# Early up-projections: the high part behind a group's first exponentials, the low part at the start of its second call

## The chip, the cores and the metric

One core of one Trainium2 chip runs the whole program. The metric is device time in microseconds (us) of one execution; the median of the runs counts. TensorE is called PE, its weight loads PEld, VectorE DVE, ScalarE ACT, GpSimd POOL, SyncE SP.

## What is computed

Attention with a band of 32 and 32 global rows over 4 batches of 8 heads, then two MLPs of 2304 tokens, width 512 and hidden width 2048:

```python
s_ll = np.where(np.abs(pos[:, None] - pos[None, :]) <= 32, scale * q_l @ k_l.T, -1e9)
a_l = sm(concat([scale * q_l @ k_g.T, s_ll]))       # local rows: global keys and a band
out_l = a_l @ concat([v_g, v_l])
out_g = sm(scale * q_g @ k_all.T) @ v_all            # global rows: all keys
x = concat([out_g, out_l]).reshape(2304, 512)        # heads side by side
h = x @ w_in;  x = where(h > 0, h, exp(min(h, 0)) - 1) @ w_out          # first MLP
h = x @ w_in2; x = where(h >= 1, h, where(h <= -1, 0, (h + 1)**2 / 4)) @ w_out2
```

## The kernel before

The MLP products are made with operands split into a high and a low part (xh and xl for activations, wh and wl for weights, gh and gl for the hidden layer), three products in place of one. The high part is a copy by ScalarE, the low part the difference to it by VectorE, so a low part always follows its high part.

The first stage, attention, is a loop of calls n = 0 to 25 over 24 units in groups of three: a local unit (one pair of heads of a batch), a global unit (the global rows of four heads), a local unit. Counted from 0, n divisible by 3 is a group's first call. A call issues the steps of three units at once: scores, maxima (top) and exponentials (expo) of unit n; transposes (turn: tiles pt or tg), their copies by ScalarE (copy: pT or pgT) and the products with the values (values: po or pog) of unit n - 1; division (norm on VectorE: den, then o_sb or og), transposes back on PE (back: ot or tg3) and the split into xh and xl (high on ScalarE, low on VectorE) of unit n - 2. Maxima read the scores in PSUM and write sn (with nml) for a local unit, m and nm for a global one; exponentials of a global unit read the scores (sg) in PSUM straight and write pg. Two PSUM banks hold scores, three the transposes, one the values.

All instructions of this stage are pinned: each engine runs its own in the order of the text. The order within a call is that of lines 733 to 750: scores(n), norm(n-2), turn(n-1), copy(n-1), back(n-2), high(n-2), top(n), low(n-2), expo(n), a step of weight preparation (wraw to top, rest, power, wh, wl) from n = 4 on, values(n-1), then loads (arrive).

Five up-projections of the first MLP run within this stage from n = UP_AT = 8 on, by a generator that is stepped twice a call: at its start (line 734) and ahead of the values (line 747). One up-projection takes 12 matmuls (six at n = 8, six at n = 9), the curve on ScalarE (exponential, then the Relu) at the start of n = 10, the join on VectorE late in n = 10, the high part gh on ScalarE at the start of n = 11 and the low part gl on VectorE late in n = 11. The next one begins in that same step, so the pattern repeats every three calls, n = 11 being a group's third call. The five share one PSUM bank, which the join frees. gh and gl come from pools of five buffers, g from one of two.

After the loop the engines are no longer pinned; the rest of the first MLP and the second MLP follow, planned by due times (later, catch_up), nearly all matmuls of lines 247 and 320. Down-projections of batch 0 are issued within n = 24 already, on the first three early results. In the profile, L113 is the helper that pins an instruction, so instructions of the first stage are told apart by their tiles.

Of the kernel before, what the change touches and what calls it, by code (L numbers as in the profile page):

```python
# [20 lines left out]
B, H, SL, SG, D = 4, 8, 512, 32, 64  # L21
# [9 lines left out]
KT = DM // P  # L31
# [14 lines left out]
UP_EARLY = 5  # L46
# [4 lines left out]
UP_AT = 8  # L51

UP_STEP = 6
# [13 lines left out]
def band_attention_then_two_mlps(  # L67
# [77 lines left out]
    chunks = []  # L145
    for layer in range(2):
        f = 0
# [164 lines left out]
    def down(layer, fs, j, f, gs, banks, ds):  # L312

        gh, gl = gs
        wh, wl = (w[:, KT * P:] for w in wtiles[layer, f])
        for d in ds:
            if f == fs[0]:
                banks[d] = ps_dn[d // 2].tile([P, SL], F32, tag=f"dn{d}", name="dn")
            for k, (w, g) in enumerate(((wl, gh), (wh, gh), (wh, gl))):
                eng.tensor.matmul(  # L320
                    banks[d],
                    w[:, d * P:(d + 1) * P],
                    g,
                    start=f == fs[0] and k == 0,
                    stop=f == fs[-1] and k == 2,
                )
            if f == fs[-1]:
                collect(layer, fs, j, d, banks[d])
# [40 lines left out]
    def mpool(name, bufs, **kw):  # L369
        return ctx.enter_context(tc.tile_pool(name=name, bufs=bufs, reuse_waits="tile", **kw))  # L370
# [6 lines left out]
    with ExitStack() as actx:  # L377
# [298 lines left out]
        def early_weights():  # L676

            for part in parts:
                for _ in range(3):
                    next(part, None)  # L680
                    yield

        def early_ups():

            for f, j in [(f, j) for j in range(B) for f in chunks[0][1]][:UP_EARLY]:
                u = Up(0, f, j)
                u.products(UP_STEP)
                yield
                yield
                u.products(3 * KT - UP_STEP)  # L690
                yield
                u.curve()
                yield
                u.join()
                yield
                u.high()
                yield
                u.low()

        parts = [prep(g_p, wtmp_p, 0, *part, raw_tag="wraw") for part in halves]  # L700
        sent = iter(parts)
        weights, ups = early_weights(), early_ups()

        def part(n, name):

            if 0 <= n < len(units):
                if n not in live:
                    live[n] = units[n][0](*units[n][1:])
                live[n][name]()

        def arrive(n):

            g, r = divmod(n, 3)
            p = 2 * g + 1
            if r == 1 and p + 1 < len(pairs):
                load_qk(*pairs[p + 1])
            elif r == 2 and p + 2 < len(pairs):
                load_qk(*pairs[p + 2])
            elif r == 0 and g:
                next(next(sent, iter([0])))  # L720
            while ahead and len(ahead) > 2 * len(pairs) - V_UNTIL.get(n, 4 * g + (4, 6, 7)[r]):
                load_v(*ahead.pop(0))
            if r == 0 and g and p < len(pairs):
                spread_queries(*pairs[p])
            elif r == 1 and p < len(pairs):
                spread_keys(*pairs[p])
            elif r == 2 and p + 1 < len(pairs):
                spread_keys(*pairs[p + 1])
# [1 line left out]
        ahead = [(*pair, (e,)) for pair in pairs[1:] for e in range(2)]  # L730
        live, first = {}, {}
        for n in range(len(units) + 2):
            if n > UP_AT:
                next(ups, None)
            part(n, "scores")
            part(n - 2, "norm")
            part(n - 1, "turn")
            part(n - 1, "copy")
            part(n - 2, "back")
            part(n - 2, "high")  # L740
            part(n, "top")
            part(n - 2, "low")
            part(n, "expo")
            if n >= PREP_AT:
                next(weights, None)
            if n >= UP_AT:
                next(ups, None)
            part(n - 1, "values")

            arrive(n)  # L750
            if n == len(units):

                s_ctx.close()
                ps_dn.append(mpool("ps_dn0", 1, space=PSUM))
                for f in chunks[0][1]:
                    down(0, chunks[0][1], 0, f, made[0, f, 0], first, range(KT // 2))
        for _ in weights:
            pass
        for _ in ups:
            pass  # L760
        prep_ctx.close()
        eng = free
# [13 lines left out]
    step = 0  # L776
# [24 lines left out]
    for ci, (layer, fs) in enumerate(chunks):  # L801
# [3 lines left out]
        for i, (j, f) in enumerate(order):  # L805
            if j == GR:
                u = Up(layer, f, j)
# [88 lines left out]
```

## Time and profile before

| | us |
|---|---|
| median of 3 runs (lowest to highest) | 861.51 (860.61 to 861.84) |
| the profiled execution, own time | 859.64 |
| its span, first to last instruction | 857.8 |
| PE busy in the span | 842.2 |
| VectorE busy | 580.6 |
| ScalarE busy | 431.7 |
| GpSimd busy | 27.0 |

Times in the rows count from the span's start. In a timeline a row is a run of like instructions on one engine; a bracket at its end is the engine's idle time just before it and the instruction that ended it. Matmul ends are modelled. The granted TensorE clock is full (1.00) in all stretches.

### The profile page before, as it was taken

What the parts mean: (1) busy time and instruction counts of PE and PEld (TensorE: products, weight loads), DVE (VectorE), ACT (ScalarE), POOL (GpSimd) and SP (SyncE); (2) the same over time, 40 slices, a digit from 0 to 9 for tenths busy, and PEclk for the clock granted to TensorE, in tenths of its full rate; (3) what the DMA queues carried; (4) which work ended last, traced back from release to release, by engine and by line L of the source; (5) the groups of instructions that cost most, each with busy time, mean ns of one, the idle gap of its engine ahead of it and who ended that gap; (6) DMA issues with size and microseconds to landing.
All of it is one profiled execution on the core that took longest, in us unless ns stands there. A gap on an engine that the chain in (4) does not pass through costs nothing.

```text
span 857.8 us, 14902 instructions
## 1 busy us (share of the span) xinstructions
PE 842.2 (98%) x6138; PEld 691.9 (81%) x6138; DVE 580.6 (68%) x1130; ACT 431.7 (50%) x755; POOL 27.0 (3%) x66
## 2 busy tenths in 40 slices
PE   8899999999999999999999999999999999999998
PEld 5677778888888888888888888888888888888886
DVE  5888857879437954734499896369759754845455
ACT  5778766765335534433456664355435333433332
POOL 2231200000000000000000000000000000000000
PEclk9999999999999999999999999999999999999999
DMA  8988712322101210200021112012102100000014
GB/s 278 305 267 266 239 47 99 105 92 99 50 1 49 99 50 1 98 1 1 1 98 50 50 64 84 1 50 99 49 1 80 69 0 1 1 1 0 2 62 147
DMA packets 23124, 65.45 MB, mean 76 GB/s; under 512 B 3984, under 2 KB 4240, under 8 KB 19344
## 3 DMA queue, kind: packets, MB, share of 16 engines
q1 hardware_dynamic: 22768, 64.23, 22.0%
q8 instruction: 48, 0.79, 0.4%
q10 hardware_dynamic: 288, 0.26, 0.1%
q14 instruction: 20, 0.16, 0.1%
HBM read 60.03 MB, written 4.46 MB: 75 GB/s over the span
## 4 chain that ended last, share of the span: by engine, by line
PE 96%; DMA 2%; issue 1%; ACT 1%; DVE 0%; SPq 0%
PE dn L320 40%; PE up L247 39%; PE up L244 3%; PE dn L337 3%; PE s L113 2%; PE po L113 2%; PE up L113 2%; PE pt L113 2%; PE sg L113 1%; PE pog L113 1%; PE tg L113 1%; DMA wraw<-in_w 1%; DMA v_sb<-in_vwin 1%; PE ot L113 1%; PE dn L113 1%
## 5 line engine op out<-in xcount | busy, mean ns | idle before, releaser
L320 PE MATMUL dn<-gh,wh 128*128 128x512 f32 x506 | 196.9, 389 | 0.0
L320 PE MATMUL dn<-gl,wh 128*128 128x512 f32 x506 | 196.8, 389 | 0.0
L320 PE MATMUL dn<-gh,wl 128*128 128x512 f32 x506 | 196.3, 390 | 0.0
L247 PE MATMUL up<-xh,wl 128*128 128x512 f32 x492 | 192.5, 391 | 0.0
L247 PE MATMUL up<-xl,wh 128*128 128x512 f32 x492 | 191.6, 389 | 0.0
L247 PE MATMUL up<-xh,wh 128*128 128x512 f32 x492 | 191.6, 389 | 0.0
L278 ACT ACTIVATE gh<-g 128x512 fp32r<-128x512 f32 x123 | 77.7, 632 | 118.8 <-DVE g L267 71.8
L297 DVE TENSOR_TENSOR acc<-dn,acc 128x512 f32<-128x512 f32 x128 | 84.7, 684 | 48.6 <-PE dn L320 48.4
L320 PEld LDWEIGHTS dn<-gl,wh 128*128 128x128 f32 x506 | 95.0, 188 | 19.8
L320 PEld LDWEIGHTS dn<-gh,wh 128*128 128x128 f32 x506 | 95.0, 188 | 19.5
L320 PEld LDWEIGHTS dn<-gh,wl 128*128 128x128 f32 x506 | 95.0, 188 | 19.4
L282 DVE TENSOR_TENSOR gl<-g,gh 128x512 fp32r<-128x512 f32 x123 | 84.5, 688 | 38.6 <-ACT gh L278 37.6
L247 PEld LDWEIGHTS up<-xh,wh 128*128 128x128 f32 x492 | 92.3, 188 | 19.2
L247 PEld LDWEIGHTS up<-xh,wl 128*128 128x128 f32 x492 | 92.4, 188 | 18.8
L247 PEld LDWEIGHTS up<-xl,wh 128*128 128x128 f32 x492 | 92.4, 188 | 18.7
L258 ACT ACTIVATE g<-up,half_sb 128x512 f32<-128x512 f32 (+1 forms) x69 | 47.0, 681 | 113.4 <-PE up L247 104.5
L266 DVE SCALAR_TENSOR_TENSOR g<-g 128x512 f32<-128x512 f32 (+1 forms) x69 | 46.9, 679 | 59.3 <-ACT g L258 59.2
L264 DVE SCALAR_TENSOR_TENSOR g<-up,g 128x512 f32<-128x512 f32 x64 | 43.3, 677 | 61.8 <-ACT g L255 61.8
L253 ACT ACTIVATE g<-up 128x512 f32<-128x512 f32 x64 | 37.8, 591 | 85.9 <-PE up L247 80.5
L267 DVE TENSOR_TENSOR g<-g,e 128x512 f32<-128x512 f32 (+1 forms) x69 | 46.9, 679 | 3.6
L180 ACT ACTIVATE top<-wraw 128x1024 f32<-128x1024 f32 x29 | 33.6, 1159 | 29.9 <-DMA wraw<-in_w 19.8
L255 ACT ACTIVATE g<-g,one_sb 128x512 f32<-128x512 f32 x64 | 45.9, 717 | 1.8
(112 smaller groups left out, 916.8 us busy)
## 6 DMA issues: line engine op xcount, KB each, us to landing
wraw<-in_w SPq DMA_DIRECT2D x29, 1024.0 KB, 4.8
v_sb<-in_vwin SPq DMA_DIRECT2D x32, 520.0 KB, 5.1
k_sb<-in_kT SPq DMA_DIRECT2D x16, 288.0 KB, 4.4
q_sb<-in_qT SPq DMA_DIRECT2D x16, 272.0 KB, 5.0
outT<-acc SPq DMA_DIRECT2D x16, 256.0 KB, 2.1
wraw<-in_w SPq DMA_DIRECT2D x6, 512.0 KB, 5.9
outT<-acc_rows SPq DMA_DIRECT2D x4, 64.0 KB, 2.2
mask_sb<-in_mask ACTq DMA_DIRECT2D x1, 192.0 KB, 4.1
```

Of the source, the lines that this page charges most:

```text
L113: return lambda *args, **kw: tc.keep_in_program_order(fn(*args, **kw))
L247: eng.tensor.matmul(self.ps, w, x, start=k == 0, stop=k == 3 * KT - 1)
L253: eng.scalar.activation(self.g, self.ps, AF.Exp)
L255: eng.scalar.activation(self.g, self.g, AF.Relu, bias=one_sb, scale=-1.0)
L258: eng.scalar.activation(self.g, self.ps, AF.Relu, bias=half_sb, scale=0.5)
L264: eng.vector.scalar_tensor_tensor(g, self.ps, 0.0, g, ALU.max, ALU.subtract)
L266: eng.vector.scalar_tensor_tensor(g, g, 1.0, g, ALU.min, ALU.mult)
L267: eng.vector.tensor_tensor(g, g, self.e, ALU.add)
L278: eng.scalar.activation(self.gh, self.g, AF.Copy)
L282: eng.vector.tensor_tensor(self.gl, self.g, self.gh.bitcast(F32), ALU.subtract)
L297: eng.vector.tensor_tensor(a, ps, a, ALU.add)
L320: eng.tensor.matmul(banks[d], w[:, d * P:(d + 1) * P], g, start=f == fs[0] and k == 0, stop=f == fs[-1] and k == 2,)
```

## The change

The generator early_ups is replaced by a function up_work, which the loop calls at the same two places of each call with n and a flag (begin). It derives from n and each running up-projection's number k what is due. Products, curve and join stay in their calls. The high part moves from the start of call 11 + 3k to the later place in call 12 + 3k, behind the exponentials and the weight step of a group's first call. The low part moves from the later place in call 11 + 3k to the start of call 13 + 3k, a group's second call, ahead of the division of unit n - 2; there it also stands ahead of the curve of the next up-projection in the text. The next up-projection's products used to follow the low part; they now follow nothing of this kind.

```diff
-        def early_ups():
-
-            for f, j in [(f, j) for j in range(B) for f in chunks[0][1]][:UP_EARLY]:
-                u = Up(0, f, j)
-                u.products(UP_STEP)
-                yield
-                yield
-                u.products(3 * KT - UP_STEP)
-                yield
-                u.curve()
-                yield
-                u.join()
-                yield
-                u.high()
-                yield
-                u.low()
+        early = [(f, j) for j in range(B) for f in chunks[0][1]][:UP_EARLY]
+
+        def up_work(n, begin):
+
+            for k, u in running.items():
+                step = n - UP_AT - 3 * k, begin
+                if step == (2, True):
+                    u.curve()
+                elif step == (2, False):
+                    u.join()
+                elif step == (4, False):
+                    u.high()
+                elif step == (5, True):
+                    u.low()
+            k, r = divmod(n - UP_AT, 3)
+            if not begin and 0 <= k < len(early) and r < 2:
+                if r == 0:
+                    running[k] = Up(0, *early[k])
+                running[k].products(UP_STEP)
...
-        weights, ups = early_weights(), early_ups()
+        weights, running = early_weights(), {}
...
-            if n > UP_AT:
-                next(ups, None)
+            up_work(n, True)
             part(n, "scores")
...
-            if n >= UP_AT:
-                next(ups, None)
+            up_work(n, False)
             part(n - 1, "values")
...
-        for _ in ups:
-            pass
```

## Rows read from the trace of the kernel before

**Rows 1.** The page, parts 1 and 4: busy us by engine; the chain's shares.
```profile
PE 842.2 (98%) x6138; PEld 691.9 (81%) x6138; DVE 580.6 (68%) x1130; ACT 431.7 (50%) x755; POOL 27.0 (3%) x66
...
PE 96%; DMA 2%; issue 1%; ACT 1%; DVE 0%; SPq 0%
```

**Rows 2.** Busy time by stretch: stretch, length, busy us of each engine, clock, DMA.
```profile
200.00:250.00 50.00, 50.00 (x224) 41.41 (x223) 27.43 (x39) 20.14 (x31) 0.00 (x0) 1.00 0.12 42
```

**Rows 3.** Waits of PE, 55 to 116 us: us in total, times, longest.
```profile
PE s L113 <- issue: 3.3, 7, 1.1
PE s L113 <- ACT top L113: 1.6, 1, 1.6
```

**Rows 4.** The chain in order of time, third and second calls: start, us, what.
```profile
69.75 0.44 issue
...
72.07 0.63 PE ot L113 x4
...
82.46 0.44 PE ot L113 x4
82.89 1.05 PE po L113 x64
83.94 0.18 issue
84.12 0.97 PE s L113 x26
85.09 0.90 issue
...
100.67 1.06 issue
```

**Rows 5.** Timeline of ScalarE, end of n = 15 to n = 17: start, us, instruction.
```profile
80.33 0.62 ACT L113 ACTIVATE wh<-top 128x512 fp32r<-128x512 f32 x1
80.85 0.58 ACT L113 ACTIVATE g<-up 128x512 f32<-128x512 f32 x1
...
82.09 1.07 ACT L113 ACTIVATE pT<-pt 128x512 f32<-128x512 f32 x2
83.04 0.60 ACT L113 ACTIVATE xh<-ot 128x512 fp32r<-128x512 f32 x1
83.52 0.88 ACT L113 ACTIVATE pg<-sg,nm 128x272 f32<-128x272 f32 x2
...
86.06 0.63 ACT L113 ACTIVATE gh<-g 128x512 fp32r<-128x512 f32 x1 [1.09 <-DVE g L113]
87.47 0.87 ACT L113 ACTIVATE pgT<-tg 128x512 f32<-128x512 f32 x2 [0.78 <-PE tg L113]
```

**Rows 6.** Timeline of VectorE, end of n = 15 to the start of n = 18.
```profile
79.05 0.69 DVE L113 SCALAR_TENSOR_TENSOR wl<-rest,power 128x512 fp32r<-128x512 uint32 x1
80.34 0.17 DVE L113 TENSOR_SCALAR den<-po 128x8 f32<-128x8 f32 x1 [0.60 <-PE po L113]
...
80.78 0.69 DVE L113 TENSOR_TENSOR o_sb<-po,den 128x512 f32<-128x512 f32 x1
...
82.20 0.21 DVE L113 TENSOR_SCALAR nm<-m 128x1 f32<-128x1 f32 x1
...
91.00 0.69 DVE L113 TENSOR_TENSOR gl<-g,gh 128x512 fp32r<-128x512 f32 x1
91.61 0.14 DVE L113 TENSOR_SCALAR den<-pog 128x1 f32<-128x1 f32 x1
```

**Rows 7.** Timeline of VectorE: den in the second calls n = 13 and 22.
```profile
65.13 0.17 DVE L113 TENSOR_SCALAR den<-po 128x8 f32<-128x8 f32 x1 [0.54 <-PE po L113]
...
111.28 0.17 DVE L113 TENSOR_SCALAR den<-po 128x8 f32<-128x8 f32 x1 [0.68 <-PE po L113]
```

**Rows 8.** Timeline of PE's weight loads in n = 16.
```profile
82.82 0.95 PEld L113 LDWEIGHTS po<-v_sb,pT 128*32 128x32 f32 x64 [0.17 <-ACT pT L113]
```

**Rows 9.** The page, part 3: DMA queue and kind, packets, MB, share of 16 engines.
```profile
q8 instruction: 48, 0.79, 0.4%
```

## The prediction

> **What bounds the kernel now.** I read the page first, part 1 and the chain of part 4: TensorE (PE) is busy for 98% of the span, and the chain that ended last is 96% PE [rows 1]. Such an average hides stages, so next came the table by stretch. From 120 us on PE is full (200 to 250 us: 50.00 of 50.00) [rows 2]; the change touches nothing there, and what the attention stage before it loses or gains reaches the end whole. So only the stage with the unit loop matters, and in it the calls n = 11 to 25, where the five early up-projections run. There I read what PE waits for: from 55 to 116 us the view has just two rows, both in front of scores matmuls [rows 3]. PE waits for no high part, no low part and no pgT. Then I took one group, calls n = 15 (first, local unit), 16 (second, global unit) and 17 (third, local unit), and laid the chain [rows 4], ScalarE [rows 5] and VectorE [rows 6] beside each other. The reader is to see three things. In the third call ScalarE stands 1.09 us in front of gh, waiting for the join, and after gh it idles another 0.78 us until PE has made tg [rows 5]: gh has slack there. From the end of the first call through the second, ScalarE has none: wh, g, pT, xh and pg follow each other without an idle mark [rows 5]. And PE's scores of the third call wait for pg, which needs xh before it on its queue, which needs ot, which needs o_sb from VectorE's norm [rows 4 to 6].
>
> **What the change takes away.** Five times gh (0.63 us) leaves the third call's start on ScalarE, and with it the 1.09 us wait [rows 5]; five times gl (0.68 us, 0.61 us until the next starts) leaves the third call's end on VectorE [rows 6]. Gain on the path: 0. On ScalarE the next instruction, pgT, waits for PE's tg in any case; on VectorE the next is the norm of pog, and no PE wait for it is among [rows 3]. The cover is PE's own solid queue. Were it gone, the gain would be at most 0.63 us a group.
>
> **What it adds.** I follow k = 1; its gh now stands at the end of n = 15 behind the eight exponentials and wh, and its gl is the first VectorE work of n = 16, ahead of norm(14), where the curve of k = 2 follows on ScalarE. Nothing is issued on SyncE or GpSimd and no DMA is moved; PE's order is unchanged. gh and gl have five buffers for five units, g has two, so no new buffer wait.
> (1) wh starts at 80.33 and the next at 80.85 [rows 5]. So gh would run from 80.85 to 80.85 + 0.63 = 81.48, and g, pT come 0.52 later: pT at 82.61.
> (2) VectorE ends wl at 79.05 + 0.69 = 79.74 and now idles 0.60 us until den at 80.34 [rows 6]. gl doesn't fit into that idle time, since its gh ends only at 81.48. In order, it waits until then, and den follows 0.61 us behind: some 82.12, that is 82.12 - 80.34 = 1.78 us later. This is the added wait; queued behind it are norm(14) and top(16).
> (3) Everything of the norm shifts by 1.78: o_sb ends at 80.78 + 0.69 + 1.78 = 83.25, nm at 82.20 + 0.21 + 1.78 = 84.19 [rows 6].
> (4) PE runs ot(14) at 82.46 now, 0.99 us after o_sb was there (81.47) [rows 4, 6]; that slack pays for part of the 1.78. After the change ot can't begin before 83.25. How long it then takes no row shows at this place; the bounds are 0.44 us, as in the solid stream, and 0.63 us, as where it opened after tg at 72.07 [rows 4]. I take 0.63, since that one too begins after a break, plus an estimated 0.05 us for the signal: end at 83.93. po(15) follows it instead of 82.89: 1.04 later.
> (5) xh(14) was at 83.04, held by pT ahead of it. pT's shift would allow 83.56; ot allows 83.93. So +0.89, and pg 84.41 for 83.52, with nm (84.19) there in time [rows 5].
> (6) The scores of n = 17 start now at 84.12, 0.18 us after po, as pg frees their banks [rows 4]. They would start near 85.01 by pg, po being 1.04 later: the shift is 0.89 to 1.04, and I take **0.95 us** for one group. From 0.44 and no signal time at (4) comes xh at 83.69, a shift of 0.65, the lower end.
>
> If the VectorE part of this were hidden, ScalarE's would remain: po's weight load already waits 0.17 us for pT [rows 8], and pT comes 0.52 later. That is the lower price of the same mechanism, about 0.5 us a group.
>
> **The sum.** The pattern stands four times, den at 65.13, 80.34, 95.66 and 111.28, the first and the last in [rows 7]: n = 13, 16, 19, 22. After each, all that follows moves as one, since the third and first calls are led by PE, so it adds up: 4 x 0.95 = 3.8 us. The fifth pair (k = 4) lies at the end of n = 24 and the start of n = 25; no scores are left there, and on PE down-projection products stand between the last values and the last ot. I price it at 0, with 0.7 us (gl and its gap) as its upper end. The profiled execution's own time is 859.64 us, 857.8 of it span; it would become 863.4. It lies 1.87 below the median of the runs, 861.51, so I add the sum to the median: 861.51 + 3.8 = **865.3 us**.
>
> **Where a page speaks to it.** In three of the third calls the scores stop a second time, in mid-stream, for 0.44, 0.90 and 1.06 us, put down to "issue" and not to any engine [rows 4], while a queue of kind "instruction" brought 48 packets, 0.79 MB, over the run [rows 9]. The Trainium skill, Runtime: NRT & Kernel Launch, section Instruction fetch mechanics, says that instructions are refilled in blocks of 16 KiB while the block before runs, and that crossing a block is mostly hidden. The size agrees with this trace (0.79 MB / 48 is about 16 KB); hidden it doesn't look here, and by the page's rule the gaps would be something else, nothing could be made up in them, and the sum would stay 865.3.
>
> **The rivals.**
> *Caught up in the issue gaps.* If those gaps are late instructions whose delivery is already under way when PE stands before ot, the delivery goes on during the new stand and the gaps shrink. For it: they come in mid-stream, some 2 to 3 us behind ot, with no releaser. Against: PE has come through slow transposes before ot, so its queue is as full before the new stand as after it, and delivery is asked for at a place in the program that moves along. At most 0.44 + 0.90 + 1.06 = 2.4 us come back: 3.8 - 2.4 = +1.4, **862.9 us**. Chance 0.15.
> *Faster: the third call was ScalarE's.* If it is gh, not PE, that holds the third call (pgT behind gh, pog behind pgT), taking it out gives back up to 0.63 us in each of five groups, 3.2 us: **858.3 us**, provided that gl costs nothing. That turns on one point: gh must end by 79.74, so that gl falls into the 0.60 us in which VectorE idles. Against it: ScalarE's 0.78 us idle behind gh ends on PE's tg, and wh starts at 80.33 [rows 5]. Chance 0.07.
> *It doesn't do what it says.* The engines' order could differ from the text's, with gl behind the norm: then only the 0.5 us of ScalarE can be lost, and part of that in front of ot; near **861.5 us**, with up to 2 us more. Against: the order of the rows before is the text's, instruction for instruction. Chance 0.08.
>
> **How the numbers follow.** Forecast 0.70, the others 0.15, 0.07, 0.08. About 0.2% (1.7 us, here 859.8 to 863.2) is what a measurement of this kernel can tell from no change. Slower by more than that: the forecast, and a third of the case of the issue gaps (if they give back only part): 0.70 + 0.05 = 0.75. Same: 0.10 + 0.07 = 0.17. Faster: 0.08, the rival's 0.07 and one for the rest. The forecast's own bounds are 4 x 0.65 = 2.6 and 4 x 1.04 + 0.7 = 4.9 us, and the order of the free instructions behind the stage may shift the end by an estimated 1 us. The range leaves out the two cases at 861.5 and below, takes in that of the gaps: 862.2 to 867.4.
>
> **What would show it.** In the trace after: gl directly in front of den in the second call, with an idle mark "ACT gh" of about 1.7 us; den 1.8 us behind the end of po; a PE idle mark in front of ot in n = 13, 16, 19 and 22 released by VectorE; the third call's scores about 1 us later in each group, and the stage's end some 3.8 us later, with PE full behind it. ScalarE in the third call would idle in front of pgT for longer than the 0.78. I am wrong if ot has no wait, if den stands no further from the next group's than before, or if the issue gaps vanish.

## The result, and the profile after

The changed kernel takes 868.1 us (median of 6 runs, 866.99 to 870.27) beside 861.21 for the kernel before: ratio 1.0076, 95% interval 1.0062 to 1.0089. It is slower, as forecast, but by 6.6 us (by the ratio; 6.9 between the medians) and not by 3.8. Its profiled execution took 867.85 us, 866.0 of it span. Single executions that took 1054 to 1698 us are left out of all ratios below, and no median moves by more than 0.2 us for them.

I count the loss in one stretch, from the first scores of n = 12 to the first down-projection product; ahead of it lies of the change only that gh and gl of k = 0 are gone from n = 11. In the chain before they start at 60.06 and 124.32, after at 61.85 and 132.48: 64.26 and 70.63 us, so 6.37 more. Behind it both kernels run alike (TensorE full). The 1.79 us by which n = 12 itself comes later I don't put down to the change: these scores started at 61.94 us in a second profile of the kernel before, at 60.35 and 62.18 with one part moved, and at 63.46 in the changed kernel again. In this execution PE stood for 2.30 us ("issue") ahead of the scores of n = 11, where the kernel before had stood for 1.57, and then made them at half the granted clock (0.50 from 56 to 58 us) in 2.08 us for 1.26; the new work had not begun by then.

The chain that ended last, changed kernel, in order of time (start, us, what). It answers to [rows 4 to 6], with k = 1 from 84.00 on:

```profile
83.48 0.52 ACT wh L113
84.00 0.53 ACT gh L113
...
84.56 0.69 DVE gl L113
85.25 0.09 DVE den L113
...
85.60 0.70 DVE o_sb L113
...
86.43 0.64 PE ot L113 x4
...
87.10 0.61 ACT xh L113
...
87.73 0.69 DVE xl L113
88.42 0.78 DVE rest L113
...
89.22 0.69 DVE rest L113
89.92 0.60 DVE g L113
...
90.86 0.70 DVE o_sb L113
...
91.70 0.63 PE ot L113 x4
92.32 1.39 PE up L113 x6
...
94.80 1.09 PE s L113 x64
95.89 0.60 PE pt L113 x4
...
96.51 1.09 ACT pT L113 x2
...
97.71 2.32 ACT sn L113 x8
...
104.72 1.18 PE s L113 x40
105.90 2.20 issue
108.10 0.64 PE s L113 x24
...
122.40 1.40 PE s L113 x54
123.80 0.73 issue
```

Before, this chain was almost all PE. Now the first two groups close in themselves over three engines: exponentials, wh, gh, gl, norm, ot, xh, xl, rest, join, norm, ot, then PE's up, pog, scores and pt, then pT and the next exponentials. The new work is read in it directly: gh and gl (84.00 to 85.25). And late in it stand two stops in the scores, 2.20 us in n = 20 ([rows 4] had 1.06 there) and 0.73 in n = 23.

VectorE's timeline, changed kernel, start of the second call n = 16, and its waits from 55 to 124 us (engine, line, releaser: us in total, times, longest), then PE's:

```profile
84.56 0.69 DVE L113 TENSOR_TENSOR gl<-g,gh 128x512 fp32r<-128x512 f32 x1 [2.07 <-ACT gh L113]
85.17 0.16 DVE L113 TENSOR_SCALAR den<-po 128x8 f32<-128x8 f32 x1
```

```profile
DVE gl L113 <- ACT gh L113: 7.8, 4, 2.1
...
PE ot L113 <- DVE o_sb L113: 6.3, 6, 1.2
PE s L113 <- issue: 4.5, 2, 2.3
```

Four waits for gh, 7.8 us together; six waits of ot where [rows 3] had none: four in the second calls, and two in the third calls of n = 14 and 17. Of the two waits put down to issue one is the stop in n = 20, the other the 2.30 us ahead of n = 11, before the stretch; the stop in n = 23 ends behind this window.

### The profile page after: what moved, and what is told of

Read it like the earlier page. It is cut to its first block, busy times and chain, and to the rows that moved or that the text cites. A ratio compares the mean times of both kernels' runs of the same rounds, so it can differ in the third digit from the quotient of the medians.

```text
span 866.0 us, 14902 instructions
## 1 busy us (share of the span) xinstructions
PE 843.0 (97%) x6138; PEld 692.5 (80%) x6138; DVE 583.1 (67%) x1130; ACT 431.5 (50%) x755; POOL 29.2 (3%) x66
## 4 chain that ended last, share of the span: by engine, by line
PE 90%; ACT 3%; DMA 3%; DVE 2%; issue 1%; SPq 0%
PE dn L320 40%; PE up L247 39%; PE up L244 3%; PE dn L337 3%; PE s L113 2%; ACT sn L113 1%; DMA wraw<-in_w 1%; ACT pT L113 1%; PE pog L113 1%; PE up L113 1%; PE ot L113 1%; PE pt L113 1%; DMA v_sb<-in_vwin 1%; DVE o_sb L113 1%; PE po L113 1%
```

## The experiments

"Stretch" is the one defined above; "groups" are its four parts, each from the first scores of one group's first call to the next (the last to the first down-projection).

| kernel | us | ratio to before (interval) | stretch | groups |
|---|---|---|---|---|
| before | 861.2 | | 64.26 | 15.14, 15.37, 15.55, 18.21 |
| before again | 861.58, one run | | 64.31 | 15.12, 15.16, 15.55, 18.48 |
| changed | 868.1 | 1.0076 (1.0062 to 1.0089) | 70.63 | 16.40, 16.55, 17.68, 19.99 |
| changed again | 870.1 | 1.0093 (1.0073 to 1.0113) | 72.06 | 16.13, 16.81, 19.20, 19.92 |
| low part alone moved | 862.6 | 1.0004 (0.9989 to 1.0018) | 65.00 | 15.84, 15.12, 15.12, 18.92 |
| high part alone moved | 863.9 | 1.0022 (1.0010 to 1.0033) | 66.38 | 15.85, 15.63, 15.65, 19.25 |
| low part ahead of the join | 866.3 | 1.0051 (1.0034 to 1.0068) | 68.45 | 16.38, 15.74, 15.74, 20.59 |
| high moved, low ahead of the join | 866.7 | 1.0053 (1.0036 to 1.0070) | 69.77 | 16.94, 16.25, 16.94, 19.64 |
| VectorE stalled | 869.5 | 1.0085 (1.0066 to 1.0103) | 71.56 | 16.95, 16.88, 17.27, 20.47 |
| before, shifted by 40 | 864.9 | 1.0038 (1.0023 to 1.0053) | 64.59 | 15.88, 15.53, 15.23, 17.95 |
| changed, shifted by 40 | 868.1 | 1.0075 (1.0057 to 1.0092) | 68.73 | 16.41, 16.55, 16.87, 18.91 |
| changed, shifted by 14 | 867.9 | 1.0068 (1.0044 to 1.0093) | 72.52 | 16.85, 16.12, 19.40, 20.14 |
| short loop | 861.3 | 0.9984 (0.9966 to 1.0002) | 65.21 | 15.20, 16.00, 15.32, 18.69 |
| short loop, shifted by 52 | 867.0 | 1.0049 (1.0030 to 1.0068) | 66.70 | 16.14, 16.84, 15.68, 18.04 |

The stretch comes from one execution each, the time from several (but for "before again"). For the kernel shifted by 14 the stretch is from a further execution of 870.17 us.

**Which of the two moves costs?** Both parts in other places, against the changed kernel:

```diff
-                elif step == (5, True):
+                elif step == (5, False):
                     u.low()
```

> The changed kernel, but the low part is issued in the second call's later place, so behind the norm, the maxima and the exponentials, not ahead of them; the high part stays behind the first call's exponentials. Before: 861.2 us, changed: 868.1. Theory V (the loss is made by VectorE waiting for gh ahead of the norm): the mark 'gl <- ACT gh' is gone, den stands right behind po again, ot in the second call has no wait or one of at most 0.3 us, and the time is 861 to 863.5 us; what is left is ScalarE's 0.52 us a group. Rival S (the loss is gh's place on ScalarE, between the exponentials and the copies, where ScalarE has no idle time): 867 to 869 us, as in the changed kernel.

Measured: 866.7 us. gl waits for nothing and den follows po again, yet only a third of the loss is gone by the ratios, and 0.86 of 6.37 us of the stretch; I had expected 861 to 863.5. The time lies 0.3 us under the range of rival S (867 to 869), too little to decide on it; the high part alone does that below. The later place in the second call puts gl ahead of the join (at 89.55 in its chain, the join behind it at 90.15), so this kernel lengthened VectorE's way from xl to the third call's norm. That this way had no slack was the first sign that the picture of the third call was wrong. The parts had to be taken singly.

The low part alone at the start of the second call, the high part where it was before the change:

```diff
-                elif step == (4, False):
+                elif step == (3, True):
                     u.high()
```

> Only the low part is moved: it is the first VectorE work of the second call, as in the changed kernel, while the high part stays at the start of the third call, two calls earlier. Theory V: gh is long made, so gl falls into the 0.60 us in which VectorE idled for po; den moves by under 0.1 us; 860 to 862 us. Rival S expects the same. Rival P (gl's place ahead of the norm costs by itself, waiting or not): four times 0.6 us, 863.5 us or more.

862.6 us, 0.6 above the range, but with a ratio of 1.0004: no loss that can be measured. Rival P falls. gl's place ahead of the norm is free if gh is long made; it lies in VectorE's idle 0.60 us [rows 6]; behind gl at 82.17 VectorE still idles 0.26 us until den.

VectorE held up without touching ScalarE (against the changed kernel; the tile gl is allotted once):

```diff
-                elif step == (4, False):
+                elif step == (3, True):
                     u.high()
+                elif step == (3, False):
+                    u.low()
                 elif step == (5, True):
-                    u.low()
+                    for _ in range(4):
+                        u.low()
```

> High and low part where they were before the change; at the start of the second call VectorE makes the low part four times over (the same numbers into the same tile), waiting for nothing: 4 x 0.61 = 2.44 us from 79.74 on, so that den comes at 82.18, 1.84 us later than before, as in the changed kernel (1.78 by my working). ScalarE is left alone. Theory V: the same loss as the change, 866 to 869 us, with ot's wait for o_sb near 1 us in each group. Rival S: 861 to 863 us.

869.5 us, 0.5 above the range of theory V and far from that of rival S, which is no proof of V: four low parts are 9.8 us of VectorE work more over the stretch, the chain runs through VectorE nearly without a break, and the loss (7.3 us of stretch) is that of a full engine. It shows how little room VectorE has there.

**The loop.** After these I formed theory L: a loop through ScalarE and VectorE as long as PE's own group. Two kernels put one piece each into it. The high part alone (against the changed kernel; the fifth low part stays in n = 25):

```diff
-                elif step == (5, True):
+                elif step == (6, False) or (k, n) == (4, 25) and not begin:
                     u.low()
```

> The high part where the change puts it; the low part where it stood before within a call, the end of a third call, but one group later (the fifth in the second call n = 25), so VectorE's order in the second call and up to the third call's norm is as before the change. Theory L: only gh's 0.52 us lies in the loop, 4 x 0.52 = 2.1 us: 863.5 to 865 us. Theory of the prediction (PE leads the third call, slack pays for ScalarE's part): at most 0.5 us a group as well, but VectorE's share absent: 861.5 to 863.5.

863.9 us, as theory L has it, but only 0.4 above the other range, so the time doesn't decide. The groups say more: beside the kernel with the low part alone, whose second and third groups took 15.12 us, they are 0.01, 0.51, 0.53 and 0.33 us longer, and gh takes 0.52 us of the chain. Not "at most": all of it, in two groups. Beside the kernel before, whose groups hold longer stops, they are 0.71, 0.26, 0.10 and 1.04 us longer, so this reading hangs on which kernel it is set beside. Rival S falls: with gh in the changed place and gl out of the way a loss of 1.9 us is left by the ratio, at most 2.8 by its interval.

The low part alone, in front of the join (high part at (3, True), low part at (5, False)):

> The high part where it was before the change; the low part in the later place of the second call, behind rest and ahead of the join, waiting for nothing. Theory L: gl's 0.61 us lies in the loop between xl and the third call's norm: 4 x 0.61 = 2.4 us, 863.5 to 865.5 us, with ot of the third call waiting for o_sb. Theory of the prediction (the third call is TensorE's, VectorE has slack there): no loss, 861 to 862.5 us.

866.3 us, over both ranges. Beside the low part alone the groups are 0.54, 0.62, 0.62 and 1.67 us longer: three times about gl's 0.61, as theory L says, and in the last group 1 us more. Of that a stop of 0.72 us in the scores of n = 21 is 0.26 longer than in that kernel, and the transposes of n = 24 take 2.26 us for 1.02, at the pace of the exponentials, which begin only at 126.95 us.

The kernel before, profiled again, shows the loop and PE trading places:

> The kernel before once more. If its issue gaps belong to the program, they stand again before matmuls 13, 27 and 41 of the scores of n = 14, 17 and 20, with 0.4 to 1.3 us, none over 2, and the stretch from the scores of n = 12 to the first down-projection takes 64 to 65.5 us: the loss of 2 us by longer gaps is then the change's. If a gap of over 2 us stands here too, it is chance. 859.5 to 863 us.

861.58 us, and the stretch of 64.31 is inside its range. Stops of 0.62 and 1.06 us stand again before the 27th and 41st matmul of n = 17 and 20, and none is over 2 us; the one of n = 14 is missing. The chain of that execution:

```profile
61.94 1.09 PE s L113 x64
63.02 0.60 PE pt L113 x4
...
63.65 1.09 ACT pT L113 x2
...
64.85 2.32 ACT sn L113 x8
67.16 0.52 ACT wh L113
67.68 0.49 ACT g L113
...
68.92 0.97 ACT pT L113 x2
69.89 0.50 ACT xh L113
...
70.41 0.69 DVE xl L113
71.10 0.35 DVE rest L113
...
71.47 0.69 DVE rest L113
72.17 0.60 DVE g L113
...
73.11 0.70 DVE o_sb L113
...
73.95 0.63 PE ot L113 x4
74.58 1.39 PE up L113 x6
...
77.06 1.08 PE s L113 x64
...
86.98 0.62 issue
...
102.32 1.06 issue
```

From 61.94 to 77.06 the chain goes round through ScalarE and VectorE in 15.12 us; the next group, to 92.22, goes through PE alone with a stop of 0.62, in 15.16. Both ways are equally long before the change. A chain shows only the one that came last, by hundredths of a microsecond.

This loop accounts for the changed order almost to the hundredth. From the end of wh to the start of xl it takes 2.73 us here (67.68 to 70.41) and 3.73 with the change (84.00 to 87.73): 1.00 us more. To this comes what VectorE's two steps named rest (0.42 and 0.69 us) take longer in a group's third call: 0.29 and 0.43 us in the first two groups of the changed kernel. 15.12 + 1.00 + 0.29 = 16.41 and 15.12 + 1.00 + 0.43 = 16.55; measured 16.40 and 16.55. The sum comes out within 0.02 us for all nine groups of the four traces of the changed order in which no stop follows (the first and second groups, and the third group of the kernel shifted by 40).

**The stops in the scores.** The warm-up matmuls at the start of the program were made narrower and more, so that everything behind stands further back in TensorE's order:

```diff
-WARM_UP = 10
+WARM_UP = 50
...
-            eng.tensor.matmul(idle, zeros[:, 0:P], zeros)
+            eng.tensor.matmul(idle[:, 0:64], zeros[:, 0:P], zeros[:, 0:64])
```

On the kernel before:

> The kernel before with 50 narrow warm-up matmuls (64 columns) in place of 10 of 512, so that the whole rest of TensorE's program stands 40 matmuls, 80 instructions, further back. Theory I (the issue gaps in the third call's scores are blocks of instructions that come late): the gaps leave matmuls 12, 26 and 40 of the scores of n = 14, 17 and 20 and stand 40 matmuls earlier in the order, mostly in the values behind ot, where TensorE has consumed fewer instructions since its last slow work, and they shrink or vanish; 858.5 to 861 us. Rival: they belong to the scores themselves (banks, keys, queries): they stay at their matmuls, 861 us.

The stops left the scores of n = 14, 17 and 20. So their place goes with the position in the program, as blocks of instructions do, and not with banks, keys or queries. But the expected gain didn't come: the time is 3.3 us longer, most of it ahead of n = 12 (63.4 us for 60.1 and 61.9), and the stretch is 64.59 us, no shorter, since ot now waits for o_sb (3.2 us, four times). The loop took over at once. The time misses both expectations.

On the changed kernel:

> The changed kernel with the 50 narrow warm-up matmuls of the shifted kernel before (864.9 us, stretch of 64.59 us from the scores of n = 12 to the first down-projection, no issue gap in the scores). If the change's loss over the loop's 4 x 1.01 us is issue gaps, then without them it is 4.0 to 4.5 us: the stretch 68.6 to 69.1 us, the time 868.5 to 869.5 us. If not: a loss of 6.5, 871 us or more.

868.1 us, just under the range; its stretch is 68.73, inside its range: **4.14 us** more than the shifted kernel before. That is the loss without stops in the scores, against 4 x 1.00 from the loop. That the two sums meet so closely is in part luck: by groups the loss is 0.53, 1.02, 1.64 and 0.96, since rest was slow in other calls of the two kernels. PE's waits from 60 to 128 us are ot for o_sb alone (7.8 us, seven times).

The changed kernel a second time:

> The changed kernel once more, to see which of its losses repeat: 866.5 to 869 us. From the first scores of n = 12 to the first down-projection it took 70.63 us, 6.37 more than before. If the loop through ScalarE and VectorE sets the pace (theory L: exponentials, wh, gh, gl, norm, ot, xh, xl, rest, join, norm, ot and round again through TensorE), the groups take about 16.5 us again. If the 2.20 and 0.73 us issue gaps of n = 20 and 23 were chance, they differ and the stretch comes to 69 to 69.5; if they belong to the change, they stand at the same place with 0.7 us or more each.

870.1 us, above the range. The stops stand at the same matmuls again, with 2.24 us in n = 20 (after 40 scores matmuls), and 0.66 us in n = 23; so they aren't chance. A third time with everything shifted by 14 matmuls (24 of 256 columns for warm-up):

> The changed kernel with 24 warm-up matmuls of 256 columns in place of 10 of 512, so that the program behind them stands 14 matmuls further back. In both profiles of the changed kernel the scores of n = 20 stopped 2.2 to 2.5 us before their 41st matmul, n = 23 stopped 0.7 to 0.9 us before the 55th, while n = 14 and 17 (13th and 27th) had no stop behind the wait in front of ot. Theory I (the place of a block of instructions within the third call decides): everything moves by one group; n = 20 stops no longer (27th), n = 23 stops for about 2.2 us before its 41st. Rival (the loads or buffers of n = 20 themselves): the stop of 2.2 us stays in n = 20. Time 866 to 870 us by both.

867.9 us. The trace that is read is that of one more execution:

> The kernel shifted by 14 matmuls once more, for a trace at full clock. Theory I: no stop in the scores of n = 20 behind the wait in front of ot, a stop of about 2.2 us before the 41st matmul of the scores of n = 23. Rival: the stop of 2.2 us stays in n = 20. 864 to 870 us.

870.17 us. Its chain:

```profile
104.97 0.97 PE s L113 x26
105.94 2.37 issue
...
124.37 1.19 PE s L113 x40
125.56 0.87 issue
```

Half of each theory. The place moved by 14 matmuls, from behind the 40th to behind the 26th in n = 20, and from the 54th to the 40th in n = 23. The length didn't move with it: n = 20 keeps its 2.2 to 2.4 us, n = 23 its 0.7 to 0.9, while n = 14 and 17 have none. Loads during the stop don't explain the length in n = 20: before the change, too, the DMA engines were busy for 0.73 of n = 20 (99.49 to 106.11 us), and in n = 23 of the changed kernel hardly a load is under way (0.02 from 120 to 125 us).

The packets of the queue of kind "instruction" [rows 9], 16 KB each, say more about n = 20. In the DMA view of the kernel before one of them starts between 99.20 and 100.67 us, ahead of the stop; with the change none starts from 98 to 105.90 us and one in the stop itself, between 105.90 and 108.10. Before, the packet started at 99.25, 1.42 us ahead of the stop at 100.67, and PE went on at 101.73, 2.48 us behind the packet's start. With the change it started at 105.91, when the stop had begun (105.90), and PE went on at 108.10, 2.19 us behind it. In the two further traces it started at 107.36 and 105.98, for stops from 107.50 and 105.94, and PE went on 2.39 and 2.33 us behind it. The packet itself took as long as before (0.95 us for 0.99). So the long stop goes with a packet that starts late, and not with a slow one. Why it starts late in the changed order stays open. Loads ahead of it are a rival that no run moved alone: with the change the DMA engines were busy for 0.88 to 0.99 of every microsecond from 102 to 106, before for 0.76 and 0.82 of the two ahead of the packet (97 to 99).

**A version better than both?** Theory L says where to cut: take rest, rest and the join out of the way from ot to ot. Against the changed kernel, in short: the weight step behind abs split so that rest goes with the third call's step, and

```diff
             part(n - 2, "norm")
+            if (n - UP_AT - 3) % 3 == 0 and (n - UP_AT - 3) // 3 in running:
+                running[(n - UP_AT - 3) // 3].join()
...
-                elif step == (2, False):
-                    u.join()
-                elif step == (4, False):
+                elif step == (3, False):
                     u.high()
```

> Against the kernel before: the loop through ScalarE and VectorE is shortened. In the third call VectorE does the norm first and the join behind it, rest and rest come with the next step of the weights a call later, gh stands behind the third call's exponentials (where ScalarE waits 1.1 us for pt) and gl at the start of the second call (0.6 us idle). Theory L: 1.05 + 0.6 us leave the loop from ot to ot, so TensorE's own order with its issue gaps sets the pace, 14.3 us of work and 0.2 to 1.3 of gaps a group for 15.1 to 15.5: 859 to 861.5 us. If VectorE or ScalarE is full in the third call instead, 862 us or more.

861.3 us, inside the range, ratio 0.9984 (0.9966 to 1.0002): 6.8 us better than the changed kernel, but not to be told from the one before. In its profile, an execution of 864.08 us, the waits of ot for o_sb are gone, and PE waits 3.1 us in front of and within scores over the stretch (and 2.5 ahead of n = 11): the stops seem to have become the bound. But the stretch is 0.95 us longer than before, so the shorter loop itself gained nothing that these runs show. Moving the stops as well:

> The short loop with 62 narrow warm-up matmuls, 52 more than before, so that the ends of instruction blocks leave the scores of the third calls. Theories L and I together: 14.3 to 14.7 us a group, 2 to 3 us less than the kernel before in the stretch from n = 12 on; the shift of 40 cost the kernel before some 3 us ahead of n = 12, and if this one does too, the time is 860 to 862 us, else 857 to 859.

867.0 us, a miss: the scores have no stop, but n = 12 begins only at 68.25 us, stops stand within pog and po instead (2.5 and 1.4 us), and the granted clock fell to half three times. No version beat the kernel before by more than its uncertainty.

## Why the forecast was right in kind and too small

**Right, and to size.** gl waited for gh ahead of the norm: forecast about 1.7 us of waiting, measured 7.8 / 4 = 1.95. den late by 1.78 us: with 3.05 us of shift by then (75.20 to 78.25 for the scores of n = 15), 80.34 becomes 83.39, and den stood at 85.17, so 1.78. ot took 0.63 to 0.64 us behind its wait, as I took it. The scores of the third call came 1.00, 1.00, 0.99 and 0.89 us later within their groups (n = 17: 84.12 + 3.05 = 87.17, measured 88.17): 3.88 us for the 3.8 of the sum. The fifth pair cost next to nothing, as priced: of the 0.90 us by which the last part grew, 0.17 are left beside its stop of 0.73.

**Wrong.** The step that failed is the one behind "The sum": after each second call "all that follows moves as one, since the third and first calls are led by PE". From the third call's scores to the next group it took 6.15, 6.38 and 6.55 us before and 6.41, 6.56 and 7.69 after; the last part, to the first down-projection, 9.11 and 10.01. That is 0.26 + 0.18 + 1.14 + 0.90 = 2.48 us, and with the 3.88 the 6.37 but for rounding. In its place the runs show a loop through ScalarE and VectorE of 15.12 us, as long as PE's own group (15.16), which the change lengthens by 1.00 us and by what rest takes longer. Two errors lie in the step.
- In n = 14 and 17 the third call was not PE's alone. I read [rows 3], in which PE waits for nothing of VectorE, as slack on VectorE; but there the norm's o_sb ended at 71.92 and ot began at 72.07. The issue gaps of 0.44 and 0.90 us did go away, as the first rival has it (and as the forecast named as a sign of being wrong), and paid nothing, since ot then stood 1.10 us waiting for o_sb in n = 14. Beyond the shift, rest took longer there, 0.98 for 0.69 us in n = 14 and 0.85 for 0.42 in n = 17, while GpSimd copied keys (72.19 to 73.84 and from 87.71). One row of before and three of after, n = 14:

```profile
71.23 0.69 DVE L113 TENSOR_TENSOR o_sb<-po,den 128x512 f32<-128x512 f32 x1
```

```profile
72.19 1.65 POOL L113 TENSOR_SCALAR k_sb<-k_sb 128x512 f32<-128x512 f32 x2 [9.12 <-DMA k_sb<-in_kT]
72.38 0.98 DVE L113 SCALAR_TENSOR_TENSOR rest<-wraw,rest 128x512 uint32<-128x512 uint32 x1
75.14 0.63 PE L113 MATMUL ot<-eye_sb,o_sb 128*128 128x128 f32 x4 [1.10 <-DVE o_sb L113]
```

- In n = 20 and 23 the stops grew by 1.14 us and by most of 0.90. I had let them stand still or shrink. The runs show that this repeats (2.20, 2.24, 2.37 us) and needs the change (1.06 twice before, 0.51 and 0.58 with one part moved). The long one is an instruction packet that starts as the stop begins; why it does so in the changed order isn't settled.

**The rivals.** The gaps were the right place to doubt, with the wrong sign. "Faster" had no ground: ScalarE's idle time in front of pgT rose from 3.5 to 10.6 us in total (55 to 124 us), so pgT waited for PE and not for gh. The order was that of the text.

**The clock.** Behind the long stop in n = 20 PE may lose more. Busy time by stretch, changed kernel again (stretch, length, busy PE, PEld, VectorE, ScalarE, GpSimd, granted clock, DMA):

```profile
108.00:109.00 1.00, 0.00 (x0) 0.00 (x0) 0.97 (x4) 0.00 (x0) 0.56 (x2) 1.00 0.75 281
...
110.00:111.00 1.00, 1.00 (x25) 0.62 (x10) 0.13 (x1) 0.00 (x0) 0.00 (x0) 0.50 0.00 0
111.00:112.00 1.00, 1.00 (x6) 1.00 (x6) 1.00 (x11) 0.10 (x1) 0.00 (x0) 0.50 0.17 29
```

PE stood still for 2.24 us, having waited for ot shortly before, and then got 0.50 of its clock, 1.2 GHz for 2.4; scores, transposes and the next ot ran at that. This group took 19.20 us, in the shifted one 19.40, and without the drop 17.68. It happened at this place in two of the three profiles of the changed order that stop there; in the first one the clock stayed at 1.00 behind a stop of 2.20 us. So it may account for some 1.5 us of scatter between its runs.

## What to carry to other kernels

That an engine waits for nothing doesn't mean the others have slack: a chain shows the way that came last, and a second way can be as long to a hundredth. Before pricing a move at nothing, follow the loop of the moved engine round once (here exponentials to exponentials over three engines) and compare its length with the group's, above all where the leading way contains stops that a delay elsewhere would swallow. A follower may be moved ahead of critical work only if what it reads is ready then: gl alone cost nothing there, behind a late gh it cost a microsecond a group.

## What the runs showed of the hardware

- TensorE stops in mid-stream at fixed distances in its program: before the change after 12, 26 and 40 scores matmuls in successive groups. 14 matmuls more at the program's start moved the places by 14, 40 more moved the two that are still seen by 38. Each of the stops in the scores of n = 14, 17, 20 and 23 in the traces of the kernel before and of the changed one ends 2.2 to 2.7 us after a 16 KB packet of the queue of kind "instruction" started. The Trainium skill, Runtime: NRT & Kernel Launch, section Instruction fetch mechanics, calls the crossing of a 16 KiB block of instructions mostly hidden. By place and by these packets the stops fit blocks of instructions, but they are not hidden here: 0.3 to 2.4 us, where 64 values matmuls go through in 1.05 us, 16 ns each. That PE waits for this packet is read from the times; no run changed the fetch alone.
- VectorE's two rest steps in the loop (128x512) took up to 0.87 us for 0.42 and up to 1.12 for 0.69. In no trace were they longer there without GpSimd at work at the same time, though not every such overlap made them longer. That GpSimd is the cause is not shown; no run moved its work alone.
- A delay on one engine didn't simply add to these stops or hide them: they vanished in two groups and more than doubled in a third.
